# Fixing the place of four small operations on GpSimd and ScalarE from the tenth chunk on

## The chip, the cores and the metric

The kernel runs on one core of a Trainium2 chip. Its five engines (TensorE for matrix products, VectorE, ScalarE, GpSimd, and SyncE, which issues transfers) each work through a list of instructions in a fixed order; they meet only where one waits for another's result. The metric is the device time of one execution in microseconds (us). Before the change it is 552.18 us, the median of three runs (550.71 to 553.72).

## The reference, cut to what matters

Two parts follow each other. The first is a gated linear attention (an mLSTM) over 4 batches, 8 heads and 768 steps with head dimension 40; for each step t

```python
m_new  = maximum(f[t] + m, i[t])
f_stab = exp(f[t] + m - m_new);  i_stab = exp(i[t] - m_new)
C = f_stab * C + i_stab * outer(v[t], k[t])
n = f_stab * n + i_stab * k[t]
y[t] = sigmoid(o_gate[t]) * (C @ q[t]) / maximum(abs(n @ q[t]), 1.0)
```

The second is a dense block over the 3072 rows of y, 320 wide, with 1536 inner columns:

```python
out = ((x @ w_a) * (x @ w_b)) @ w_out
```

## The kernel before, in words

**Chunks.** The 768 steps are cut into six stretches of 128; a stretch of one batch with its eight heads is a chunk, so there are 24 chunks, numbered 0 to 23 in the order stretch by stretch. Batch and stretch of chunk n are `n % 4` and `n // 4`. Inside a chunk the recurrence is written as masked matrix products: scores of queries against keys (`pS`), times a matrix E of decays (one 128 x 128 block for each head), times the values (`pV`), plus a part from the state carried over (`pI`). Products that need full precision are made of several bf16 parts ("high", "middle", "low").

**Steps of one chunk.** The function `attention` goes through the chunks and in each through the letters B, D, E, A, C, U, F:

- B (`stage_b`, twice, for four heads each, then `stage_i`): scores on TensorE (L544), E times the scores on VectorE (L549), its high part cast to bf16 on ScalarE (L551, "the P cast"), the middle and low parts on VectorE (L553, L555); the state's part (L570, L574).
- D (`stage_d`) of the chunk before: the gated result y is transposed on TensorE (L709) and split into two parts (L713, L714), the dense block's input. In every fourth chunk the output gates of the next stretch are loaded here (L208, 4 transfers) and put through a sigmoid on ScalarE (L218).
- E (`stage_e`) of the next chunk: its E begins as a copy of gate sums spread over all partitions (`gbc`, a transfer of 512 KB, issued at L225); GpSimd masks it (L485, one instruction for all heads), ScalarE takes eight exponentials, one for each head (L492).
- A (`stage_a`, then `stage_v`) of the next chunk: queries and keys are split in three parts (L510, L515, L520, L521 on ScalarE, L514, L517 on VectorE), and transposed by transfers that SyncE issues (L524, four for each chunk). Values are split in three parts by two subtractions on GpSimd (L531, then L533).
- C (`stage_c`): values weighted for the state on GpSimd (L584), E times values on TensorE (L603), sums on VectorE and GpSimd (L610, L614).
- U (`stage_u`): the state's update (L630, L637, L641), its parts (L648, L649, L654, L655) and their way through device memory (L658 to L661); it also issues the load of the gate sums two chunks ahead.
- F (`stage_f`): the denominator on VectorE (L671 to L673), the gate times its reciprocal on GpSimd (L686, "the gate's product"), times the numerator on VectorE (L687), and a copy of the last columns on ScalarE (L688).

**The dense block.** Chunks are gathered into nine blocks of two or three (`sizes`); `moe_block` runs twelve inner slices for each: 16 products "up" (L812), then on VectorE and ScalarE a copy, a product and two parts (L818, L819, L821, L823), and, two slices later, the products "down" (L783). While block kb runs through the dense part, the attention of block kb + 2 is traced between its pieces.

**Order.** The start of the kernel is written out in a fixed order. All that follows is put in order on each engine by the compiler's planner, which runs the traced program through a model of the machine and issues what becomes ready there first. The order found there is what the chip then follows, whatever comes late on the chip. `tc.issue_after(x)` adds one constraint: what is traced in the block, on the engine of x, comes behind x in that engine's list. It is an order alone, not a wait.

**Names for the step that is moved.** `after["p"]` is set at L686 and holds the gate's product of the chunk whose F was traced last; before the change it is set and never read. When `stage_e` and `stage_v` of chunk n are traced, in the middle of chunk n - 1, the last F traced is that of chunk n - 2. `stage_b` of chunk n - 1 has already been traced then, with both its P casts.

Of the kernel before, what the change touches and what calls it, by code (L numbers as in the profile page):

```python
# [14 lines left out]
AF = mybir.ActivationFunctionType  # L15
ALU = mybir.AluOpType
# [4 lines left out]
def kernel(  # L21
# [13 lines left out]
    nc = tc.nc  # L35
    B, H, S, D = q.shape
    DM, DFF = w_a.shape
    P = 128
# [54 lines left out]
    for j in range(3):  # L93
# [4 lines left out]
        mask, mask, pattern=[[1, P]], compare_op=ALU.is_ge, fill=-1e30, base=0, channel_multiplier=-1  # L98
# [6 lines left out]
    x = ident[0:BH, 0:BH].rearrange("k (x j) -> k x j", j=2)  # L105
# [20 lines left out]
    after = {}  # L126
# [101 lines left out]
    def top(x):  # L228

        return x.bitcast(BF16).rearrange("p h (d w) -> p h d w", w=2)[:, :, :, 1]  # L230
# [98 lines left out]
    def beta_col(c, b):  # L329
        return g_col(c, b, 0)  # L330
# [149 lines left out]
    def stage_e(n):  # L480

        c, b = chunks[n]
        E = gbc.pop(n)
        st.setdefault(n, {})["E"] = E
        nc.gpsimd.affine_select(  # L485
            E, E, pattern=[[0, H], [1, P]], compare_op=ALU.is_ge, fill=-1e30, base=0,
            channel_multiplier=-1,
        )
        yield
        beta = beta_col(c, b)  # L490
        for h in range(H):
            nc.scalar.activation(E[:, h], E[:, h], AF.Exp, bias=beta[:, h:h + 1])  # L492
            if h % 2 == 1:
                yield

# [32 lines left out]
    def stage_v(n):  # L528
        s = st[n]
        x, vr, vl = (v3[n % NQ][:, i] for i in range(3))  # L530
        nc.gpsimd.tensor_tensor(vr, x, top(x), op=ALU.subtract)  # L531
        yield
        nc.gpsimd.tensor_tensor(vl, vr, top(vr), op=ALU.subtract)  # L533
        yield

    def stage_b(n, hf):
        s = st[n]
        qT, kT = s["T"]
        pS = ps_at.tile([P, HH, P], F32, tag="pat", name=f"pS{n}_{hf}")
        K3 = 3 * D  # L540
        for x in range(HH):
            h = hf * HH + x
            for w in range(2):
                nc.tensor.matmul(  # L544
                    pS[:, x, :], kT[0:K3, w, h, :], qT[0:K3, w, h, :], start=(w == 0), stop=(w == 1)
                )
        yield
        E = s["E"][:, hf * HH:(hf + 1) * HH]
        nc.vector.tensor_tensor(E, pS, E, op=ALU.mult)  # L549
        pb = apool.tile([P, 2, HH, P], BF16, tag="pb", name=f"pb{n}_{hf}")  # L550
        nc.scalar.copy(pb[:, 0], E)  # L551
        yield
        nc.vector.tensor_tensor(E, E, pb[:, 0], op=ALU.subtract)  # L553
        mid = E.bitcast(BF16).rearrange("s h (t w) -> s h t w", w=2)[:, :, :, 1]
        nc.vector.tensor_tensor(pb[:, 1], E, mid, op=ALU.subtract)  # L555
        s[f"pb{hf}"] = (pb[:, 0], mid, pb[:, 1])
        yield
# [108 lines left out]
    def stage_f(n):  # L666
        s = st[n]
        num = s["num"]
        nq = num[:, :, D]
        den = apool.tile([P, H], F32, tag="den", name=f"den{n}")  # L670
        nc.vector.tensor_scalar(den, nq, -1.0, 1.0, op0=ALU.mult, op1=ALU.max)  # L671
        nc.vector.tensor_tensor(den, nq, den, op=ALU.max)
        nc.vector.reciprocal(den, den)  # L673
        yield
        c, b = chunks[n]
        y = osig[c][:, b]
        yv = y[:, 0:DM].rearrange("p (h d) -> p h d", h=H)
        if n < NS:
            t = apool.tile([P, H * DV], F32, tag="tmp", name=f"y{n}")[:, 0:DM]
            t = t.rearrange("p (h d) -> p h d", h=H)  # L680
            nc.vector.tensor_tensor(t, num[:, :, 0:D], den.unsqueeze(2).broadcast_to([P, H, D]), op=ALU.mult)
            nc.vector.tensor_tensor(yv, t, yv, op=ALU.mult)
            nc.scalar.copy(y[:, DM:], y[:, 2 * P:DM])
            s["y"] = y
            return
        after["p"] = [nc.gpsimd.tensor_tensor(yv, yv, den.unsqueeze(2).broadcast_to([P, H, D]), op=ALU.mult).ins]  # L686
        nc.vector.tensor_tensor(yv, num[:, :, 0:D], yv, op=ALU.mult)  # L687
        nc.scalar.copy(y[:, DM:], y[:, 2 * P:DM])  # L688
        s["y"] = y
        yield  # L690
# [31 lines left out]
    def attention():  # L722
        for n in range(NS, NCH):
# [4 lines left out]
            for o in "BDEACUF":  # L728
# [8 lines left out]
                elif o == "B":  # L737
                    yield from stage_b(n, 0)
                    yield from stage_b(n, 1)
                    yield from stage_i(n)  # L740
                elif o == "D":
                    if n > NS:
                        yield from stage_d(n - 1)
                    if n % B == 0 and n > 0:
                        load_o(n // B)
                elif o == "E":
                    if n + 1 < NE:
                        yield from begin_e(n + 1)
                    elif n + 1 < NCH:
                        yield from stage_e(n + 1)  # L750
                elif o == "A":
                    if n + 1 < NCH:
                        yield from stage_a(n + 1)
                        yield from stage_v(n + 1)
                elif o == "U":
                    if NE <= n + 2 < NCH:
                        load_g(n + 2)
                    u = stage_u(n)
                    yield next(u, None)
                    late.append(u)  # L760
                    if len(late) > 2:
                        yield from late.pop(0)
                else:
                    yield from {"C": stage_c, "F": stage_f}[o](n)
# [186 lines left out]
    with tc.tile_pool(name="spool", bufs=3) as spool:  # L951
# [4 lines left out]
        def start():  # L956
# [57 lines left out]
            signs(2)  # L1014
            run(begin_c(1))
            run(stage_f(0))
            words(2)
            run(stage_u(0))
            load(NS + 2)
            weigh(1)  # L1020
            leading(2)
            signs(3)
            run(stage_f(1))
            d0, d1 = stage_d(0), stage_d(1)
            warm = ps_dn.tile([P, 512], F32, tag="pd2", name="warm2")
# [34 lines left out]
    def rest():  # L1060
        if NS < NE:
            yield from begin_e(NS)
        if NS < NF32:
            yield from begin_a(NS)
        else:
            yield from stage_a(NS)
            yield from stage_v(NS)
        if NS >= NE:
            yield from stage_e(NS)
        yield from attention()  # L1070
# [49 lines left out]
```

## Time and profile before

| | |
|---|---|
| median of three runs | 552.18 us (550.71 to 553.72) |
| profiled execution: its own time / span | 551.88 us / 550.1 us |
| granted TensorE clock, mean | 0.994 |
| busy: TensorE, VectorE, ScalarE, GpSimd | 537.8, 411.6, 269.2, 149.5 us |
| masks L485 | 20, 23.4 us busy |
| exponentials L492 | 160 and 5 table loads, 49.4 us busy |
| first subtraction on values L531 | 18, 15.2 us busy |
| gate's product L686 | 22, 18.2 us busy |

The span is the time from the first to the last record of the profile. A row of the timeline gives the start, the duration, the engine, the line of the kernel, the operation and, in square brackets, how long the engine had been idle before it and what ended that. "PE" is TensorE, "PEld" its loading of weights, "DVE" VectorE, "ACT" ScalarE, "POOL" GpSimd, "SPq" SyncE's queue.

### The profile page before, as it was taken

Reading aid. Unit: us, or ns where it says so; the run is one execution under the profiler, and the core shown is the slowest. Engines: PE = TensorE matmul, PEld = TensorE weight load, DVE = VectorE, ACT = ScalarE, POOL = GpSimd, SP = SyncE. Lnnn points to the kernel's source line nnn. Section 1 sums busy time; section 2 is a strip of 40 time slices with the busy share of each in tenths; the row PEclk is TensorE's granted clock in tenths of the full one; section 3 lists DMA queues with packets and bytes.
Section 4 is the critical chain, followed back from the end, with each engine's and each line's share of the span. In section 5 each row is a group of like instructions: output and inputs, shape, how many; then the busy total and the mean of one; then the engine's idle time right before and its main releaser. Section 6 shows DMA issues by size and latency. Waiting matters only on the chain.

```text
span 550.1 us, 11947 instructions
## 1 busy us (share of the span) xinstructions
PE 537.8 (98%) x4493; PEld 511.4 (93%) x4493; DVE 411.6 (75%) x906; ACT 269.2 (49%) x645; POOL 149.5 (27%) x224
## 2 busy tenths in 40 slices
PE   8999999899999999999999999999999899999997
PEld 5888888799999999999999999999999899999996
DVE  6889999977768785988868974988677846964332
ACT  5574488664425853645625664655354813321111
POOL 3102324545032340442233340444041203210000
PEclk9799999999999999999999999999999999999999
DMA  9999943284537665668646885758459403300001
GB/s 190 217 220 284 323 88 71 64 179 113 89 100 142 139 128 113 133 131 179 121 119 115 127 161 116 140 123 170 91 130 183 102 1 104 78 1 24 1 1 36
DMA packets 198549, 66.71 MB, mean 121 GB/s; under 512 B 184220, under 2 KB 191772, under 8 KB 198492
## 3 DMA queue, kind: packets, MB, share of 16 engines
q1 hardware_dynamic: 198444, 65.86, 56.6%
q8 instruction: 35, 0.57, 0.5%
q14 instruction: 22, 0.18, 0.1%
q10 hardware_dynamic: 48, 0.10, 0.0%
HBM read 41.11 MB, written 5.95 MB: 86 GB/s over the span
## 4 chain that ended last, share of the span: by engine, by line
PE 80%; DVE 6%; DMA 4%; ACT 4%; issue 2%; SPq 2%; POOL 0%; ACTq 0%; DVEq 0%; POOLq 0%
PE pu L812 42%; PE pd L783 20%; PE pU L630 3%; PE pV L603 3%; PE pS L544 3%; DMA T<-qks 2%; DMA osig<-in_o_gate_dram 1%; PE pX L709 1%; PE pV L929 1%; ACT gbc L492 1%; PE pI L570 1%; PE pS L886 1%; PE warm L961 1%; SPq L524 1%; PE pc L451 1%
## 5 line engine op out<-in xcount | busy, mean ns | idle before, releaser
L812 PE MATMUL pu<-xh,w 128*128 128x384 f32 (+1 forms) x1080 | 273.2, 322 | 1.5 <-DVE w L459 0.7
L812 PE MATMUL pu<-xl,w 128*128 128x384 f32 (+1 forms) x648 | 206.1, 320 | 0.0
L812 PEld LDWEIGHTS pu<-xh,w 128*128 128x128 f32 x1080 | 188.3, 188 | 4.0 <-DVE w L459 1.3
L783 PE MATMUL pd<-w,gh 128*128 128x320 f32 x576 | 127.2, 311 | 0.2 <-DVE gh L821 0.2
L812 PEld LDWEIGHTS pu<-xl,w 128*128 128x128 f32 x648 | 121.8, 188 | 0.0
L819 DVE TENSOR_TENSOR g<-pu,g 128x384 f32<-128x384 f32 (+1 forms) x108 | 54.4, 504 | 82.8 <-PE pu L812 47.6
L783 PEld LDWEIGHTS pd<-w,gh 128*128 128x128 f32 x576 | 96.3, 188 | 0.6 <-DVE gh L821 0.4
L818 ACT COPY g<-pu 128x384 f32<-128x384 f32 (+1 forms) x90 | 39.6, 440 | 103.3 <-PE pu L812 96.0
L783 PE MATMUL pd<-w,gl 128*128 128x320 f32 x288 | 84.7, 311 | 0.0
L614 POOL TENSOR_TENSOR num<-v,num 128x168 f32<-128x168 f32 x36 | 21.3, 593 | 210.3 <-DVE v L610 209.7
L823 DVE TENSOR_TENSOR gl<-g,gh 128x384 fp32r<-128x384 f32 (+1 forms) x92 | 57.3, 622 | 2.0
L492 ACT ACTIVATE gbc<-gbc,gtab 128x128 f32<-128x128 f32 x160 | 49.4, 390 | 12.3 <-POOL gbc L485 12.2
L783 PEld LDWEIGHTS pd<-w,gl 128*128 128x128 f32 x288 | 52.7, 188 | 0.2
L821 DVE CAST gh<-g 128x384 fp32r<-128x384 f32 (+1 forms) x108 | 42.2, 390 | 1.7
L515 ACT CAST qks<-r 128x320 bf16<-128x320 f32 x36 | 16.4, 458 | 30.1 <-DVE r L514 30.0
L610 DVE TENSOR_REDUCE v<-pV 128x168 f32<-128x504 f32 x36 | 24.1, 675 | 9.2 <-PE pV L603 9.1
L485 POOL TENSOR_SCALAR_AFFINE_SELECT gbc<-gbc 128x1024 f32<-128x1024 f32 x20 | 23.4, 1171 | 24.7 <-DMA gbc<-g_dram 23.3
L584 POOL TENSOR_TENSOR vw<-va,gtab 128x336 f32<-128x336 f32 x20 | 17.0, 852 | 47.5 <-PE pU L630 22.2
L553 DVE TENSOR_TENSOR gbc<-gbc,pb 128x512 f32<-128x512 f32 x36 | 25.4, 707 | 4.5 <-ACT pb L551 4.5
L520 ACT COPY qks<-qks 128x640 bf16<-128x640 bf16 x36 | 26.1, 725 | 0.7
L549 DVE TENSOR_TENSOR gbc<-pS,gbc 128x512 f32<-128x512 f32 x36 | 24.3, 679 | 1.7 <-PE pS L544 1.7
L551 ACT CAST pb<-gbc 128x512 bf16<-128x512 f32 x36 | 22.2, 617 | 5.7 <-DVE gbc L549 5.6
(152 smaller groups left out, 810.1 us busy)
## 6 DMA issues: line engine op xcount, KB each, us to landing
gbc<-g_dram SPq DMA_DIRECT2D x20, 512.0 KB
q<-in_q_dram SPq DMA_DIRECT2D x24, 160.0 KB
k<-in_k_dram SPq DMA_DIRECT2D x24, 160.0 KB
va<-in_v_dram SPq DMA_DIRECT2D x24, 160.0 KB
osig<-in_o_gate_dram SPq DMA_DIRECT2D x24, 160.0 KB
raw<-in_moe_w_out_dram SPq DMA_DIRECT2D x12, 320.0 KB
out_dram<-o SPq DMA_DIRECT2D x24, 160.0 KB
raw<-in_moe_w_a_dram SPq DMA_DIRECT2D x8, 384.0 KB
```

Source lines behind the costliest of these rows:

```text
L485: nc.gpsimd.affine_select(E, E, pattern=[[0, H], [1, P]], compare_op=ALU.is_ge, fill=-1e30, base=0, channel_multiplier=-1,)
L492: nc.scalar.activation(E[:, h], E[:, h], AF.Exp, bias=beta[:, h:h + 1])
L520: nc.scalar.copy(qks[:, 0, :, lo:lo + 2 * D], qks[:, 1, :, D - lo:3 * D - lo])
L549: nc.vector.tensor_tensor(E, pS, E, op=ALU.mult)
L553: nc.vector.tensor_tensor(E, E, pb[:, 0], op=ALU.subtract)
L610: nc.vector.tensor_reduce(t, pv.rearrange("p h i d -> p h d i"), axis=mybir.AxisListType.X, op=ALU.add)
L783: nc.tensor.matmul(pd[t][:, 0:DM], a[:, cols], w, start=(ff == 0 and first), stop=(ff == NF - 1 and last),)
L812: nc.tensor.matmul(acc[j], a, r, start=(x == 0), stop=(x == len(terms) - 1),)
L818: (nc.vector.tensor_copy if ff in [1, 2] else nc.scalar.copy)(g, acc[0])
L819: nc.vector.tensor_tensor(g, acc[1], g, op=ALU.mult)
L821: nc.vector.tensor_copy(gh, g)
L823: (nc.gpsimd if kb * 12 + ff < 16 else nc.vector).tensor_tensor(gl, g, gh.bitcast(F32), op=ALU.subtract)
```

## The change

From chunk 9 on (`n > 2 * B`, B = 4, so for the fifteen chunks 9 to 23) three things are put in a fixed place in their engine's list. The mask of chunk n (L485) and the first subtraction on its values (L531) are issued on GpSimd behind the gate's product of chunk n - 2. The eight exponentials of chunk n (L492) are issued on ScalarE behind the P cast of the second four heads of chunk n - 1 (L551). No instruction is added or taken away, and all data, waits and buffers are as before.

```diff
@@ stage_e(n)
-        nc.gpsimd.affine_select(
-            E, E, pattern=[[0, H], [1, P]], compare_op=ALU.is_ge, fill=-1e30, base=0,
-            channel_multiplier=-1,
-        )
+
+        fixed = n > 2 * B
+        with tc.issue_after(after["p"]) if fixed else nullcontext():
+            nc.gpsimd.affine_select(
+                E, E, pattern=[[0, H], [1, P]], compare_op=ALU.is_ge, fill=-1e30, base=0,
+                channel_multiplier=-1,
+            )
         yield
         beta = beta_col(c, b)
         for h in range(H):
-            nc.scalar.activation(E[:, h], E[:, h], AF.Exp, bias=beta[:, h:h + 1])
+            with tc.issue_after(after["pb"]) if fixed else nullcontext():
+                nc.scalar.activation(E[:, h], E[:, h], AF.Exp, bias=beta[:, h:h + 1])
@@ stage_v(n)
-        nc.gpsimd.tensor_tensor(vr, x, top(x), op=ALU.subtract)
+        with tc.issue_after(after["p"]) if n > 2 * B else nullcontext():
+            nc.gpsimd.tensor_tensor(vr, x, top(x), op=ALU.subtract)
@@ stage_b(n, hf)
-        nc.scalar.copy(pb[:, 0], E)
+        after["pb"] = nc.scalar.copy(pb[:, 0], E).ins
@@ stage_f(n)
-        after["p"] = [nc.gpsimd.tensor_tensor(yv, yv, den.unsqueeze(2).broadcast_to([P, H, D]), op=ALU.mult).ins]
+        after["p"] = nc.gpsimd.tensor_tensor(yv, yv, den.unsqueeze(2).broadcast_to([P, H, D]), op=ALU.mult).ins
```

## The prediction

> **What bounds the kernel now.** I read the page's busy shares first.
>
> ```profile
> PE 537.8 (98%) x4493; PEld 511.4 (93%) x4493; DVE 411.6 (75%) x906; ACT 269.2 (49%) x645; POOL 149.5 (27%) x224
> ```
>
> TensorE (PE) is busy for 98% of the span. The change touches GpSimd (27%) and ScalarE (49%) alone, and only from chunk 9, whose mask is the sixth on GpSimd's timeline:
>
> ```profile
> 162.78 1.36 POOL L485 TENSOR_SCALAR_AFFINE_SELECT gbc<-gbc 128x1024 f32<-128x1024 f32 x1 [1.22 <-DMA gbc<-g_dram]
> ```
>
> So the question is how much PE is idle behind that point. The table of busy time by stretch answers it; the first column is PE, and the other engines follow.
>
> ```profile
> core 0: us, PE busy (x) PEld busy (x) DVE busy (x) ACT busy (x) POOL busy (x), PEclk, DMA share, GB/s
> 160.00:240.00 80.00, 80.00 (x703) 76.78 (x702) 65.68 (x136) 43.69 (x105) 27.09 (x38) 1.00 0.64 134
> 240.00:260.00 20.00, 19.41 (x175) 18.52 (x175) 16.23 (x34) 12.75 (x29) 8.64 (x13) 1.00 0.80 165
> 260.00:420.00 160.00, 160.00 (x1366) 154.99 (x1363) 123.22 (x260) 83.53 (x206) 48.91 (x65) 1.00 0.68 131
> 420.00:440.00 20.00, 18.55 (x146) 17.95 (x145) 16.64 (x33) 14.87 (x32) 6.17 (x8) 1.00 0.63 138
> 460.00:480.00 20.00, 19.81 (x212) 19.04 (x211) 19.48 (x48) 8.24 (x22) 7.66 (x10) 1.00 0.42 101
> 480.00:500.00 20.00, 20.00 (x168) 19.94 (x168) 11.82 (x29) 5.12 (x13) 1.82 (x3) 1.00 0.05 18
> ```
>
> PE is idle for 20 - 19.41 = 0.59 us, then 20 - 18.55 = 1.45 us, then 20 - 19.81 = 0.19 us: together 2.23 us, 0.4% of the time, in all the stretch where attention work is left for the change to move. The clock is at 1.00 in each. Everything else that PE lost lies ahead of chunk 9. The view of who waited for whom, for PE, names the three places:
>
> ```profile
> PE pX L709 <- DVE gbc L549: 1.4, 1, 1.4
> PE pS L544 <- DMA T<-qks: 1.1, 2, 0.6
> PE pd L783 <- DVE gh L821: 0.2, 1, 0.2
> ```
>
> **The change part by part.** It adds no instruction, no transfer and no wait; fifteen masks, fifteen subtractions and 120 exponentials get a later place. A typical chunk from the timelines of GpSimd, VectorE and ScalarE, at chunk 13's E (the product belongs to chunk 11, the casts to chunk 12):
>
> ```profile
> 242.56 1.21 POOL L485 TENSOR_SCALAR_AFFINE_SELECT gbc<-gbc 128x1024 f32<-128x1024 f32 x1 [1.45 <-DMA gbc<-g_dram]
> 243.75 1.02 POOL L686 TENSOR_TENSOR osig<-osig,den 128x320 f32<-128x320 f32 x1
> 242.00 0.18 DVE L673 RECIPROCAL den<-den 128x8 f32<-128x8 f32 x1
> 244.11 0.68 DVE L549 TENSOR_TENSOR gbc<-pS,gbc 128x512 f32<-128x512 f32 x1
> 245.74 0.68 DVE L549 TENSOR_TENSOR gbc<-pS,gbc 128x512 f32<-128x512 f32 x1
> 262.93 0.68 DVE L549 TENSOR_TENSOR gbc<-pS,gbc 128x512 f32<-128x512 f32 x1
> 243.81 2.46 ACT L492 ACTIVATE gbc<-gbc,gtab 128x128 f32<-128x128 f32 x8 [1.02 <-POOL gbc L485]
> 246.75 0.61 ACT L551 CAST pb<-gbc 128x512 bf16<-128x512 f32 x1
> 247.79 0.62 ACT L551 CAST pb<-gbc 128x512 bf16<-128x512 f32 x1
> ```
>
> *The mask and the subtraction.* The denominator is ready at 242.00 + 0.18 = 242.18, but the product runs at 243.75, since the mask stands in front of it and itself waited 1.45 us for its transfer. Behind the change the product can run at 242.2: 1.55 us earlier. The mask then ends near 242.2 + 1.02 + 1.21 = 244.4 instead of 243.77, so 0.7 us later. What waited behind the mask was the product, and behind that VectorE's L687 and ScalarE's copy L688; what is late next is the exponentials. The subtraction L531 stood behind the product here already.
>
> *The exponentials.* They start at 243.81 and hold ScalarE for 2.46 us; behind them queue the next keys' cast (L510), both P casts and L688. VectorE finishes the first product with E at 244.11 + 0.68 = 244.79, so the first cast can come some 2 us earlier, and with it L553 and L555. The exponentials move behind the second cast, to about 245.74 + 0.68 + 0.62 = 247.0, and end at 249.5. Who waits for them is the next chunk's L549, at 262.93: 13 us of cover. Were that gone, the cost would be what the exponentials are late by, 249.5 - 246.27 = 3.2 us, in each chunk, and PE would only pay it where it has no dense products to run.
>
> So in each chunk a chain of small operations gets 1.5 to 2.5 us shorter, and PE, which is full, gains nothing from it. The gain can come at the three idle places only.
>
> *First place, 0.59 us.* PE waits for chunk 13's transposes. From the timelines of SyncE's queue and ScalarE:
>
> ```profile
> 249.02 2.71 SPq L208 DMA_DIRECT2D osig<-in_o_gate_dram  x4
> 251.77 5.54 SPq L524 DMA_TRANSPOSE T<-qks  x3
> 255.47 1.28 ACT L218 ACT_TABLE_LOAD   x1 [4.96 <-DMA osig<-in_o_gate_dram]
> ```
>
> Three transposes stand behind the four gate loads. Both hang on work that the exponentials hold up (the loads on chunk 11's y, transposes on the keys' parts). If both start the 1.5 to 2.5 us earlier that was found above, the 0.59 us go. The exponentials' new time, 247 to 249.5, lies ahead of the 4.96 us in which ScalarE idles for the gates. Bounds: 0 where the queue's order stays and the loads are no earlier, -0.59. I take -0.59, as 1.5 us is well over it.
>
> *Second place, 1.45 us.* PE waits at 431 us for VectorE's L549, which frees the score bank:
>
> ```profile
> 427.12 0.72 POOL L686 TENSOR_TENSOR osig<-osig,den 128x320 f32<-128x320 f32 x1 [2.37 <-ACT osig L218]
> 427.79 1.09 POOL L485 TENSOR_SCALAR_AFFINE_SELECT gbc<-gbc 128x1024 f32<-128x1024 f32 x1
> 431.93 0.68 DVE L549 TENSOR_TENSOR gbc<-pS,gbc 128x512 f32<-128x512 f32 x1
> ```
>
> Here the mask already stands behind the product, which was late because of the sigmoid (2.37 us of waiting), and this L549 waits for no exponential of the next chunk. The change removes nothing in front of it. Bounds 0 and -1.45; I take 0.
>
> *Third place, 0.19 us, and the fifteenth chunk.* In the narrow block near 465 us VectorE is busy for 19.48 of 20 us, and PE waits for its L821:
>
> ```profile
> 463.46 1.35 POOL L485 TENSOR_SCALAR_AFFINE_SELECT gbc<-gbc 128x1024 f32<-128x1024 f32 x1 [1.56 <-DMA gbc<-g_dram]
> 464.79 0.74 POOL L531 TENSOR_TENSOR va<-va 128x336 f32<-128x336 f32 x1
> 465.61 1.08 POOL L533 TENSOR_TENSOR va<-va 128x336 f32<-128x336 f32 x1
> 467.89 1.06 POOL L686 TENSOR_TENSOR osig<-osig,den 128x320 f32<-128x320 f32 x1 [1.21 <-DVE den L673]
> 476.76 0.69 DVE L549 TENSOR_TENSOR gbc<-pS,gbc 128x512 f32<-128x512 f32 x1 [0.28 <-PE pS L544]
> ```
>
> Here the mask and both subtractions ran 3 us ahead of the product and now come behind it, from 468.95 to 468.95 + 1.35 + 0.74 + 1.08 = 472.1. Chunk 23's exponentials follow the mask and end near 470.3 + 2.46 = 472.8, still 4 us ahead of the L549 that needs them. While GpSimd works, VectorE is slower (rows at rival A). With GpSimd quiet until 467.9, VectorE reaches L821 earlier and PE's 0.19 us go; the slowness comes again behind 469. Bounds -0.19 and +3.17 (the three operations' whole time laid on PE); I take -0.19, as the table shows no idle PE in the 20 us that follow.
>
> **Sum:** 551.88 - 0.59 - 0 - 0.19 = 551.10 us for the profiled execution. That execution lies 0.30 us under the median of the runs shown (552.18), so the median should be 551.4.
>
> **The rivals.** *A: GpSimd's work lands on a full VectorE.* Two rows show what one mask does to VectorE:
>
> ```profile
> 304.30 1.25 POOL L485 TENSOR_SCALAR_AFFINE_SELECT gbc<-gbc 128x1024 f32<-128x1024 f32 x1 [1.41 <-DMA gbc<-g_dram]
> 304.64 1.32 DVE L823 TENSOR_TENSOR gl<-g,gh 128x384 fp32r<-128x384 f32 x1
> 296.61 0.56 DVE L823 TENSOR_TENSOR gl<-g,gh 128x384 fp32r<-128x384 f32 x1
> ```
>
> L823 begins inside the mask, ends at 305.96, 0.41 us behind the mask's end at 305.55, and takes 1.32 instead of 0.56 us. Where VectorE has no slack, such a delay reaches PE through L821 and L823. It has none near 470 us, where the change puts 3.17 us of GpSimd's work: 551.88 + 3.17 + 0.30 = 555.35 us. It decides where VectorE's lateness passes what PE has in hand, and PE already waits for L821 in this stretch. Against it: the same 3.17 us are taken from 463 to 467, so the load is only moved. The Trainium skill (SBUF — State Buffer, "SBUF: two separate sides") says that the two engines share one pair of ports as an exclusive lock, held for a whole instruction, while the other blocks; by that rule the mask costs VectorE up to its full duration wherever it lands, and the sum would be this rival's. The rows just shown agree with the lock.
>
> *B: PE's pieces come together in other ways.* When both score halves run at once they cost less than apart. From the chain in order of time and PE's timeline:
>
> ```profile
> 242.67 0.91 PE pS L544 x16
> 285.33 0.55 PE pS L544 x8
> 289.51 0.46 PE pS L544 x8
> 305.17 0.42 PE L812 MATMUL pu<-xh,w 128*128 128x384 f32 x1
> 306.64 0.34 PE L812 MATMUL pu<-xh,w 128*128 128x384 f32 x1
> ```
>
> Apart: 0.55 + 0.46 = 1.01 against 0.91, and one more first "up" product behind a switch, 0.42 against 0.34: 0.18 us a chunk, at most 2.7 us for fifteen. With an earlier cast and E used sooner, the planner may draw the halves together. With half of that and all three idle places gone: 551.88 - 2.23 - 1.35 + 0.30 = 548.6 us. Against it: PE's order depends on much that the change does not touch, and it may as well part halves that are together now.
>
> *C: the shift is swallowed.* The chains get shorter, the queue's order in front of PE does not change, all three waits stay: 552.2 us. For it: the two waits that matter end on transposes and on VectorE, neither of which the change moves itself.
>
> **How the numbers follow.** About 0.5% (2.8 us) is what a measurement of this kernel can tell from no change, its three runs being 3 us apart. The forecast has 0.42, C 0.15: both within 0.5%. B has 0.18 and is faster, since the three idle places alone (0.4%) do not get there. A, and any order of the planner that leaves PE waiting as long, has 0.25 and is slower. The range goes from a little under B (548.3) to a little over A (555.6); the likeliest case's own is 549.9 (all 2.23 us) to 552.8.
>
> **What would show it.** Product L686 ahead of mask L485 on GpSimd in all fifteen chunks, and no longer held by the mask's transfer; eight exponentials behind two P casts, and the casts right behind L549; no PE wait on transposes near 258 us; the 1.4 us wait of L709 still there; PE busy near 538 us. The forecast is wrong if PE's idle time behind 160 us grows past 4 us (then A, with waits on L821 or L819, or a new one), or if PE's busy time itself falls by over 1 us (B).

## The result, and the profile after

The changed kernel is slower: a median of 555.09 us (553.25 to 558.74) against 551.94 us (549.95 to 554.93) for the kernel before, fourteen runs of each. The ratio is 1.006, with a 95% interval of 1.0036 to 1.0085. Executions that took far longer than the rest are left out of every ratio, and f1 below has no idle time because its profile is of such an execution. The profiled execution took 555.12 us, its span 553.3 us.

In the rows from here on the lines of the kernel stand three to five higher than before: mask L488, exponentials L496, subtractions L536 and L538, scores L549, E times scores L554, P cast L556, middle and low parts L558 and L560, product of the gate L691, numerator L692, casts of the transposed y L718 and L719, transposes of y L714, "down" L788, "up" L817, the dense block's copy L823, and its two parts L826 (gh) and L828 (gl).

The page of the changed kernel, busy time by engine:

```profile
PE 536.6 (97%) x4493; PEld 509.1 (92%) x4493; DVE 417.2 (75%) x906; ACT 270.6 (49%) x645; POOL 152.0 (27%) x224
```

No engine has more instructions, yet VectorE is busy for 5.6 us more. TensorE (PE) is what sets the time, so the table of busy time by stretch comes next, with the columns shown before (behind the length of the stretch, the first is PE and the sixth the granted clock):

```profile
160.00:240.00 80.00, 78.45 (x673) 75.22 (x672) 63.99 (x130) 44.07 (x105) 27.09 (x35) 1.00 0.60 132
240.00:260.00 20.00, 20.00 (x193) 18.83 (x192) 18.58 (x40) 9.79 (x25) 9.18 (x14) 1.00 0.64 133
260.00:420.00 160.00, 159.34 (x1352) 153.40 (x1352) 125.14 (x260) 84.93 (x202) 51.08 (x67) 1.00 0.64 133
420.00:440.00 20.00, 19.52 (x161) 18.54 (x159) 15.44 (x30) 14.63 (x32) 6.31 (x8) 1.00 0.80 159
440.00:460.00 20.00, 19.40 (x125) 19.40 (x126) 7.76 (x16) 4.84 (x13) 0.00 (x0) 1.00 0.00 1
460.00:480.00 20.00, 19.27 (x197) 18.52 (x196) 17.88 (x40) 8.22 (x22) 7.00 (x9) 1.00 0.49 125
```

PE's idle time from 160 to 480 us is 1.55 + 0 + 0.66 + 0.48 + 0.60 + 0.73 = 4.02 us, where it was 2.23 us. Place by place, in PE's timeline: the 0.59 us near 258 are gone and the 1.45 near 431 are down to 0.22; 1.52 near 203, 0.66 near 273 and 0.86 near 440 (it begins before 440 and so falls into two stretches) are new, and the 0.19 near 469 have become 0.73 near 472. The view of who waited for whom names what PE waits for there:

```profile
PE pX L714 <- DVE gbc L554: 1.7, 2, 1.5
PE pu L817 <- ACT g L823: 1.5, 2, 0.9
PE pd L788 <- DVE gh L826: 0.7, 1, 0.7
```

The second row is a wait that the kernel before did not have in this part: PE waits for ScalarE's copy of an "up" product. The timelines of ScalarE, TensorE and VectorE show why, first near 273 us (exponentials of chunk 14), then near 440 (chunk 22):

```profile
269.05 1.28 ACT L496 ACT_TABLE_LOAD   x1
270.34 2.47 ACT L496 ACTIVATE gbc<-gbc,gtab 128x128 f32<-128x128 f32 x8
272.72 0.45 ACT L519 CAST qks<-r 128x320 bf16<-128x320 f32 x1
273.06 0.47 ACT L823 COPY g<-pu 128x384 f32<-128x384 f32 x1
...
273.59 0.45 PE L817 MATMUL pu<-xh,w 128*128 128x384 f32 x1 [0.66 <-ACT g L823]
...
289.35 0.68 DVE L554 TENSOR_TENSOR gbc<-pS,gbc 128x512 f32<-128x512 f32 x1
...
436.06 1.28 ACT L496 ACT_TABLE_LOAD   x1
437.36 2.47 ACT L496 ACTIVATE gbc<-gbc,gtab 128x128 f32<-128x128 f32 x8
439.73 0.44 ACT L514 CAST qks<-q 128x320 bf16<-128x320 f32 x1
440.08 0.47 ACT L823 COPY g<-pu 128x384 f32<-128x384 f32 x1
...
440.60 0.44 PE L817 MATMUL pu<-xh,w 128*128 128x384 f32 x1 [0.86 <-ACT g L823]
```

The eight exponentials stand as one block behind the second P cast. For a chunk that follows a sigmoid, a load of ScalarE's function table (ACT_TABLE_LOAD) stands in front of them: together 3.8 us. Behind the block stands the copy that empties a bank (a buffer that PE's products land in) of "up" products, and PE wants that bank. The row of VectorE shows the first product that needs chunk 14's exponentials, 16 us behind their end.

The wait near 203 us is on VectorE (timelines of VectorE and TensorE, the changed kernel, then the same two before):

```profile
199.65 0.62 PE L549 MATMUL pS<-T,T 120*128 120x128 bf16 x8
...
200.07 0.68 DVE L554 TENSOR_TENSOR gbc<-pS,gbc 128x512 f32<-128x512 f32 x1
...
201.43 1.03 DVE L692 TENSOR_TENSOR osig<-num,osig 128x320 f32<-128x320 f32 x1
202.38 1.23 DVE L558 TENSOR_TENSOR gbc<-gbc,pb 128x512 f32<-128x512 f32 x1
203.54 0.68 DVE L554 TENSOR_TENSOR gbc<-pS,gbc 128x512 f32<-128x512 f32 x1
...
204.27 0.55 PE L714 MATMUL pX<-ident,osig 128*128 128x128 f32 x3 [1.52 <-DVE gbc L554]
```

```profile
200.87 1.07 PE L544 MATMUL pS<-T,T 120*128 120x128 bf16 x16
...
203.87 1.27 DVE L549 TENSOR_TENSOR gbc<-pS,gbc 128x512 f32<-128x512 f32 x2
...
206.20 0.53 PE L709 MATMUL pX<-ident,osig 128*128 128x128 f32 x3
```

Before, the planner had put both halves of E times the scores together, and both halves of the scores on PE. Now two slow operations stand between the halves on VectorE. The second half, which frees the score bank, ends no later than before (204.22 against 205.14 us), but PE, whose list is redrawn too, has issued its scores earlier and comes for the bank earlier: at 206.20 us before, from 202.75 on after. So it is the two lists together that make this wait. Near 472 us it is the late product of the gate and GpSimd's work behind it (timelines of GpSimd, VectorE, TensorE, changed kernel):

```profile
469.39 0.86 POOL L691 TENSOR_TENSOR osig<-osig,den 128x320 f32<-128x320 f32 x1 [4.83 <-DVE den L678]
470.21 1.54 POOL L488 TENSOR_SCALAR_AFFINE_SELECT gbc<-gbc 128x1024 f32<-128x1024 f32 x1
...
470.72 1.57 DVE L558 TENSOR_TENSOR gbc<-gbc,pb 128x512 f32<-128x512 f32 x1
472.21 0.83 DVE L826 CAST gh<-g 128x256 fp32r<-128x256 f32 x1
...
473.10 0.70 PE L788 MATMUL pd<-w,gh 128*128 128x320 f32 x3 [0.73 <-DVE gh L826]
```

The mask lies on VectorE's L558, which takes 1.57 us there against 0.68 in most chunks, and gh comes late behind it. That the mask is what makes gh late is read from these rows and was not tried alone: e2 below, where the mask is free, waits 1.20 us for the same cast.

### The profile page after: what moved, and what is told of

Same layout as the page of the kernel before. It is cut to its first block, busy times and chain, and to the rows that moved or that the text cites. A ratio compares the mean times of both kernels' runs of the same rounds, so it can differ in the third digit from the quotient of the medians.

```text
span 553.3 us, 11941 instructions
## 1 busy us (share of the span) xinstructions
PE 536.6 (97%) x4493; PEld 509.1 (92%) x4493; DVE 417.2 (75%) x906; ACT 270.6 (49%) x645; POOL 152.0 (27%) x224
## 4 chain that ended last, share of the span: by engine, by line
PE 71%; DVE 11%; ACT 5%; issue 5%; DMA 4%; SPq 2%; POOL 1%; ACTq 0%; DVEq 0%; POOLq 0%
PE pu L817 40%; PE pd L788 19%; PE pV L608 3%; PE pS L549 2%; PE pU L635 2%; ACT gbc L496 1%; DVE cw L425 1%; PE pX L714 1%; DMA osig<-in_o_gate_dram 1%; DVE cr L428 1%; DMA T<-qks 1%; DMA c_dram<-cb 1%; DVE w L459 1%; PE pI L575 1%; DVE gh L826 1%
## 5 line engine op out<-in xcount | busy, mean ns | idle before, releaser
L817 PE MATMUL pu<-xh,w 128*128 128x384 f32 (+1 forms) x1080 | 273.8, 323 | 3.2 <-ACT g L823 1.5
L817 PE MATMUL pu<-xl,w 128*128 128x384 f32 (+1 forms) x648 | 206.4, 321 | 0.0
L817 PEld LDWEIGHTS pu<-xh,w 128*128 128x128 f32 x1080 | 188.0, 188 | 6.0 <-ACT g L823 2.1
L788 PE MATMUL pd<-w,gh 128*128 128x320 f32 x576 | 126.5, 310 | 0.7 <-DVE gh L826 0.7
L817 PEld LDWEIGHTS pu<-xl,w 128*128 128x128 f32 x648 | 121.8, 188 | 0.1
L788 PEld LDWEIGHTS pd<-w,gh 128*128 128x128 f32 x576 | 96.3, 188 | 1.1 <-DVE gh L826 0.9
L788 PE MATMUL pd<-w,gl 128*128 128x320 f32 x288 | 84.5, 311 | 0.0
L823 ACT COPY g<-pu 128x384 f32<-128x384 f32 (+1 forms) x90 | 39.7, 441 | 86.0 <-PE pu L817 78.6
L828 DVE TENSOR_TENSOR gl<-g,gh 128x384 fp32r<-128x384 f32 (+1 forms) x92 | 52.3, 568 | 1.5
L788 PEld LDWEIGHTS pd<-w,gl 128*128 128x128 f32 x288 | 52.6, 188 | 0.4 <-DVE gl L828 0.2
L496 ACT ACTIVATE gbc<-gbc,gtab 128x128 f32<-128x128 f32 x160 | 49.6, 393 | 3.9 <-POOL gbc L488 3.9
L826 DVE CAST gh<-g 128x384 fp32r<-128x384 f32 (+1 forms) x108 | 45.4, 420 | 1.6
L558 DVE TENSOR_TENSOR gbc<-gbc,pb 128x512 f32<-128x512 f32 x36 | 28.8, 801 | 4.4 <-ACT pb L556 4.4
L556 ACT CAST pb<-gbc 128x512 bf16<-128x512 f32 x36 | 22.2, 619 | 15.5 <-DVE gbc L554 15.5
L488 POOL TENSOR_SCALAR_AFFINE_SELECT gbc<-gbc 128x1024 f32<-128x1024 f32 x20 | 24.6, 1228 | 11.6 <-DMA gbc<-g_dram 10.3
L691 POOL TENSOR_TENSOR osig<-osig,den 128x320 f32<-128x320 f32 x22 | 17.7, 805 | 29.2 <-DVE den L678 18.8
```

The lines of the kernel that those rows point to most:

```text
L488: nc.gpsimd.affine_select(E, E, pattern=[[0, H], [1, P]], compare_op=ALU.is_ge, fill=-1e30, base=0, channel_multiplier=-1,)
L556: after["pb"] = nc.scalar.copy(pb[:, 0], E).ins
L788: nc.tensor.matmul(pd[t][:, 0:DM], a[:, cols], w, start=(ff == 0 and first), stop=(ff == NF - 1 and last),)
L817: nc.tensor.matmul(acc[j], a, r, start=(x == 0), stop=(x == len(terms) - 1),)
L823: (nc.vector.tensor_copy if ff in [1, 2] else nc.scalar.copy)(g, acc[0])
L826: nc.vector.tensor_copy(gh, g)
```

## The experiments

The first four kernels leave the order to the compiler's planner. The others have the list of every engine written out, taken from the kernel before or from the changed one, so that nothing moves but what the experiment moves. "Idle" in the table is PE's idle time from 160 to 480 us, 320 us less PE's busy time in that stretch of each profile. Each ratio is to runs of the kernel before on the same chip.

| kernel | median us | ratio (95%) | idle us |
|---|---|---|---|
| before | | 1 | 2.23 |
| the change | 555.09 | 1.0060 (1.0036 to 1.0085) | 4.02 |
| e1: masks and subtractions | 556.62 | 1.0075 (1.0039 to 1.0112) | 4.31 |
| e2: exponentials | 555.18 | 1.0058 (1.0037 to 1.0078) | 4.21 |
| e3: masks | 556.33 | 1.0082 (1.0061 to 1.0103) | 3.55 |
| e5: the change, exponentials of 10, 14, 18, 22 free | 558.26 | 1.0121 (1.0101 to 1.0140) | 4.88 |
| r1: lists of before, all moves | 559.48 | 1.0136 (1.0113 to 1.0160) | 7.77 |
| r1a: lists of before, GpSimd's moves | 564.23 | 1.0225 (1.0191 to 1.0259) | 9.85 |
| r1b: lists of before, exponentials | 555.31 | 1.0063 (1.0041 to 1.0086) | 4.35 |
| r2: lists after, moves put back | 577.75 | 1.0463 (1.0432 to 1.0494) | 16.23 |
| f1: r1b without chunks 14, 18, 22 | 551.38 | 0.9979 (0.9953 to 1.0006) | – |
| f2: r1b, chunks 14, 18, 22 alone | 556.21 | 1.0079 (1.0052 to 1.0107) | 4.11 |
| f3: r1 without four places | 553.42 | 1.0018 (0.9992 to 1.0045) | 2.98 |
| f4: the change, copy ahead at two places | 552.95 | 1.0014 (0.9991 to 1.0036) | 2.27 |
| f5: f4 and two repairs on VectorE | 553.90 | 1.0019 (0.9990 to 1.0049) | 2.59 |
| f6: f1 and one repair on VectorE | 552.96 | 0.9999 (0.9972 to 1.0026) | 2.05 |

### Parts of the change, as the planner draws them

e1 frees the exponentials, e2 frees mask and subtraction, e3 keeps the mask's constraint alone, and e5 takes the constraint from the exponentials that follow a sigmoid:

```diff
 e1, e3
-            with tc.issue_after(after["pb"]) if fixed else nullcontext():
+            with tc.issue_after(after["pb"]) if False else nullcontext():
 e2 (both), e3 (the subtraction's)
-        with tc.issue_after(after["p"]) ...
+        with tc.issue_after(after["p"]) if False else nullcontext():
 e5
-            with tc.issue_after(after["pb"]) if fixed else nullcontext():
+            with tc.issue_after(after["pb"]) if fixed and n % B != 2 else nullcontext():
```

> Masks and values' first subtractions of chunks 9 to 23 behind the gate's product as in the change; the exponentials free, as before. Theory G (GpSimd's mask and subtractions now run while VectorE is full, and slow it until TensorE waits): 2 to 3.5 us slower than before, with a wait of TensorE on VectorE near 470 us, and VectorE's busy time up by 3 us or more. Theory S (the exponentials, with the table load ahead of them, stand as one block of 2.5 to 3.75 us behind the second P cast and in front of the dense block's copies on ScalarE): no more than 1 us from before, and no wait of TensorE on ScalarE's copy.

> Exponentials of chunks 9 to 23 behind the second P cast as in the change; masks and subtractions free, as before. Theory S: 2 to 3.5 us slower than before, with TensorE waiting on ScalarE's copy g twice, about 0.8 and 1.0 us. Theory G: within 1 us of before, VectorE's busy time as before to 1 us.

> The masks alone behind the gate's product; subtractions and exponentials free. Theory G: slower by 1 us or more, since the mask is the longest of the three operations that move; Theory S: within 1 us of before. If the slowness comes from any new order the planner draws rather than from one part, this run has waits of TensorE at places that none of the others has.

> The whole change, but the exponentials of chunks 10, 14, 18 and 22, those that follow a sigmoid and need a table load of 1.28 us first, stay free. Theory S: the two waits of TensorE on ScalarE's copy (0.82 and 1.03 us) are gone, and the time is 1.5 to 2 us under that of the change. Theory G: as slow as the change to 0.7 us.

Each part alone costs about what the whole costs, so the parts don't add up, and e5, meant to take a cost away, is the slowest of the four. The waits lie at other places in each kernel: a constraint makes the planner draw all five lists anew. e1 came out as theory G had it (0.73 us of waiting near 472, VectorE busy for 4.0 us more). e2 has the time that theory S gave but not its waits: none is on the dense block's copy; one of 1.17 us near 437 is on ScalarE's copy L693 (L688 before), which stands behind chunk 22's block there. With the planner in between, these runs can't tell a part from its redrawing.

### The moves without the new order, and the new order without the moves

r1 keeps the lists of before and moves 25 instructions of GpSimd (13 masks, and the subtractions that stood ahead of the product; two masks stood behind it already) and 120 exponentials of ScalarE to where the change puts them. r1a and r1b each do one engine. r2 takes the lists of the changed kernel, with every mask back ahead of the product and the exponentials ahead of the first P cast. The edits for one chunk, as line numbers in an engine's list:

```diff
 r1, r1b: ScalarE, chunk 14
-L525 L519 L524 L693 exp*2 L556 exp*4 L823 exp*2 L653 L514 L556 L525 L519
+L525 L519 L524 L693 L556 L823 L653 L514 L556 exp*8 L525 L519
 r1, r1a: GpSimd, chunk 23
-L488 L536 L538 L691
+L691 L488 L536 L538
```

> Every engine's list is written out by hand as it is in the kernel before, on TensorE, VectorE and SyncE without any change; on GpSimd alone the masks (and the subtractions, where they stood ahead) are put behind the gate's product, on ScalarE alone the exponentials behind the second P cast, for chunks 9 to 23. So these are the change's moves without the order that the planner drew around them. Theory M (the moves themselves cost: GpSimd on a full VectorE, exponentials in front of copies): 2 to 3.5 us slower than before. Theory P (the cost is the order that the planner draws anew for TensorE, VectorE and SyncE): within 1 us of before, with TensorE's waits behind 160 us 3 us or less in sum.

> Every engine's list is written out by hand as it is in the changed kernel, but with each mask of chunks 9 to 23 put back in front of the gate's product on GpSimd, and each chunk's exponentials in front of the first P cast on ScalarE. So this is the new order of TensorE, VectorE and SyncE without the moves. Theory P: 2 to 4 us slower than before, like the change; some more is possible, since the lists were drawn for the other places. Theory M: within 1 us of before.

> As the lists of before with the moves alone, but only GpSimd's (25 instructions change their place), ScalarE as before. Theory M with GpSimd as the cause: 1.5 us or more slower than before, and a wait on VectorE near 470 us of 0.8 us or more. Theory P: within 1 us, VectorE's busy time within 2 us of before.

> As the lists of before with the moves alone, but only ScalarE's (120 exponentials), GpSimd as before. Theory M with ScalarE as the cause: 1.5 us or more slower than before, with waits on ScalarE's copy near 270 and 440 us. Theory P: within 1 us of before; the wait on transposes near 258 us may shrink.

The moves by themselves cost 7.6 us (559.48 against 551.92), more than the change. So the theory that only the redrawn order costs has fallen: the new order takes back more than half of what the moves cost. It does not fit the old placement, as r2 shows (25.8 us slower; why so much was not followed up). Neither theory had these sizes: r1 lies above the 2 to 3.5 us of theory M, r2 far above the 2 to 4 of theory P. In r1 PE's longest waits are on ScalarE's copy. The view of waits, then the timelines of ScalarE and GpSimd near chunk 23:

```profile
PE pu L817 <- ACT g L823: 3.7, 3, 2.3
```

```profile
469.30 0.62 ACT L556 CAST pb<-gbc 128x512 bf16<-128x512 f32 x1
473.31 2.45 ACT L496 ACTIVATE gbc<-gbc,gtab 128x128 f32<-128x128 f32 x8 [3.40 <-POOL gbc L488]
475.66 0.35 ACT L823 COPY g<-pu 128x256 f32<-128x256 f32 x1
...
471.12 1.06 POOL L691 TENSOR_TENSOR osig<-osig,den 128x320 f32<-128x320 f32 x1 [4.83 <-DVE den L678]
472.14 1.14 POOL L488 TENSOR_SCALAR_AFFINE_SELECT gbc<-gbc 128x1024 f32<-128x1024 f32 x1
```

GpSimd stands idle for 4.83 us until the denominator is there, because the mask, which could run, is now behind the product. ScalarE stands idle for 3.40 us, because the exponentials wait for the mask. The copy behind them starts as they end. PE pays for both.

### Where the exponentials' cost sits

f1 and f2 divide r1b: f1 leaves the exponentials of chunks 14, 18 and 22 where they were and moves the other twelve; f2 moves those three alone.

```diff
-for n in range(9, 24): move the exponentials of n behind the second P cast
+f1: for n in range(9, 24) if n not in (14, 18, 22)
+f2: for n in (14, 18, 22)
```

> Every engine keeps the list of the kernel before; only the exponentials of twelve chunks move behind the second P cast (not those of 14, 18 and 22, behind which the dense block's copy or the cast of x stood when all fifteen moved). Theory Q (an instruction that frees a bank of TensorE stands behind the moved block): the waits near 269 (1.5 us), 360 (1.2) and 439 us (0.6) are gone, and the 0.9 us wait on transposes near 258 stays gone, so the time is that of before within 1.5 us, 550.5 to 552.5. Rival S (the later exponentials slow VectorE and the chain everywhere, the three waits are only where it shows): 12 of 15 parts of the 3.4 us loss stay, 554 to 555.

> The complement: lists of before, and only the exponentials of chunks 14, 18 and 22 move. Theory Q: the three waits come back (about 1.5 + 1.2 + 0.6 = 3.3 us) and the wait of 0.9 us near 258 stays as before, so about 555 us. Rival S: a fifth of the loss, 552 to 553.

Twelve blocks cost nothing that can be measured (0.9979), three cost 0.8%. f6 below moves the same twelve blocks, and its profile shows none of the three waits. The wait on transposes near 258, which f2 was expected to keep, is gone there. The view of waits of f2 shows the copy of g, and xl (L719), which follows the cast of x (L718); that cast stands behind chunk 18's block:

```profile
PE pu L817 <- ACT g L823: 1.3, 2, 0.9
PE pV L608 <- DVE xl L719: 1.0, 1, 1.0
```

These three chunks follow a sigmoid (chunk 10 does too, but has no such wait), so their block is 3.8 instead of 2.5 us long. Whether the shorter block would do no harm at the same three places was not tried.

### The changed kernel with the copy ahead

f4 has the lists of the changed kernel, and f5 adds two edits on VectorE:

```diff
 f4, f5: ScalarE, chunk 14
-L556 exp*8 L519 L823
+L556 L823 exp*8 L519
 f4, f5: ScalarE, chunk 22
-L556 exp*8 L514 L823
+L556 L823 exp*8 L514
 f5: VectorE, chunk 10
-L554 L828 L692 L558 L554
+L554 L828 L554 L692 L558
 f5: VectorE, near 470 us
-L521 L560 L558 L826
+L521 L826 L560 L558
```

> Every engine keeps the list of the changed kernel; on ScalarE alone the next copy of an up product goes ahead of the exponentials of chunks 14 and 22. Theory Q: TensorE's waits on that copy (0.8 us near 273 and 1.0 near 439) go and nothing comes in their place, as the exponentials have 10 us in hand: 1.9 us less than the changed kernel, about 553.2. Rival S: the waits move to the next copy or to VectorE and the time stays at 555.

> As the kernel with the copy ahead, and on VectorE, in chunk 10, the second product of E with the scores (which frees the score bank that TensorE waits for, 1.8 us near 202) goes ahead of the numerator's product and one subtraction, and near 470 us the cast of gh (0.9 us of TensorE's waiting) ahead of two instructions of the P parts. Theory Q: 0.8 + 1.0 + 1.5 + 0.9 = 4.2 us less than the changed kernel, about 551, that is the time of before: the whole loss sits at four places. Rival S: VectorE is busy for 5.6 us more than before and hands the lateness on to whatever comes next, so under 2 us come back, 553 or more.

Two instructions moved past sixteen exponentials bring the changed kernel back to the time of before. f4's timeline of ScalarE at chunk 14, and its row for 160 to 480 us:

```profile
267.41 0.61 ACT L556 CAST pb<-gbc 128x512 bf16<-128x512 f32 x1
267.93 0.47 ACT L823 COPY g<-pu 128x384 f32<-128x384 f32 x1
268.42 1.28 ACT L496 ACT_TABLE_LOAD   x1
269.71 2.46 ACT L496 ACTIVATE gbc<-gbc,gtab 128x128 f32<-128x128 f32 x8
```

```profile
160.00:480.00 320.00, 317.73 (x2719) 306.21 (x2719) 251.48 (x518) 166.14 (x397) 100.76 (x133) 1.00 0.60 126
```

The copy could run at 267.93 and had stood at 273.06, and PE's idle time is 2.27 us against 2.23 us before. f5's edits did take the wait near 203 away, but others of 0.8 and 1.1 us in sum came near 354 and 434 us, and the 0.73 us near 472 became two waits of 0.47 and 0.12: the lateness is handed on, as the rival had it, and no gain over f4 can be measured.

### GpSimd's share, and a try at a faster kernel

f3 is r1 without the blocks of chunks 14, 18 and 22 and without any move of chunk 23. f6 is f1 with one edit against the 1.4 us wait near 431 us.

```diff
 f3: not moved
+exponentials of 14, 18, 22; mask, subtractions and exponentials of 23
 f6: VectorE, near 431 us
-L826 L521 L521 L554
+L826 L554 L521 L521
```

> Lists of the kernel before on all engines; mask, subtractions and exponentials move as in the change, but for the exponentials of chunks 14, 18 and 22 and all of chunk 23. Theory Q (GpSimd's share of the loss is the copy held up near 473 us): of the 7.6 us that all the moves cost, the waits near 269, 360, 441 and 473 (1.0 + 2.0 + 0.6 + 2.5 us, and about 1.5 us of slower matmuls behind the last) are gone, and the time is 551 to 553. Rival S (GpSimd's later work slows VectorE in every chunk): the 4.2 us between the moves on both engines and the exponentials alone stay for the most part, 555 or more.

> Lists of before, exponentials moved in twelve chunks as above, and on VectorE, near 431 us, the product of E with the scores that frees the score bank goes ahead of two subtractions of the keys' parts (0.88 us). Theory Q: of the 1.4 us for which TensorE waits there, 0.9 go, and nothing else changes: about 0.9 us under the kernel without the three blocks, 550.5, and under before. Rival S: the wait passes to the transposes of the keys behind those subtractions or to the next cast, and the time stays at 551.4.

In f3 the masks and subtractions of fourteen chunks stand behind the product (twelve of the masks were moved there), and eleven blocks of exponentials behind the casts, and that costs nothing that can be measured. So of r1's 7.6 us nearly all sat at four places. GpSimd's part of it is chunk 23, where the product is late by itself. This holds with the exponentials moved as well. In r1a they keep their old place, ahead of the P casts and the copy, and wait there for the later mask (5.13 us near 474); PE's waits on the copy are 4.9 us, and the loss is 12.3 us, which was not taken apart further. f6 did not come under the kernel before: the wait at 431 shrank, and one for gl of the same size came 2.3 us later. The view of waits of f6:

```profile
PE pX L714 <- DVE gbc L554: 0.6, 1, 0.6
PE pd L788 <- DVE gl L828: 0.6, 1, 0.6
```

No kernel here is measurably faster than before.

## Why the prediction was wrong, step by step

*What bounds the kernel* was right: PE sets the time, and PE's idle time behind 160 us goes broadly with the ratio in the table. From it the prediction drew that only the three idle places could change. That holds for a gain. A loss needs no idle place: it makes one, wherever an instruction that frees a bank for PE comes late.

*The exponentials* are the step that failed. The prediction asked who waits for the exponentials, found "13 us of cover", and named what was queued behind them at their old place (L510, the P casts, L688); the P casts now stand ahead of the block in every chunk. It did not ask what would be queued behind them at the new place. That was the dense block's copy at chunks 14 and 22, for which PE had no cover. f4 prices this step: with the lists of all other engines left alone, the two waits of 0.66 and 0.86 us go, PE's idle time falls by 1.75 us (4.02 to 2.27), and no loss is left that can be measured (1.0014, 0.9991 to 1.0036). The price that the prediction set for lost cover, "3.2 us in each chunk", hung on the next L549, which never waited for them (they end 5.1 us or more ahead of it in every chunk), and the table load of 1.28 us was in no term.

*The mask and the subtraction.* The product comes ahead of the mask in all fifteen chunks, as forecast, but not all of them are moved: 13 of the 15 masks and 7 of the 15 first subtractions stood ahead of it before. Twelve of the fifteen blocks are free in f1, and fourteen of the fifteen masks in f3. "What is late next is the exponentials" was right, and at chunk 23 in r1 that was one link of the wait of 2.3 us; the other, the copy behind the exponentials, is the same failed step.

*First place* (-0.59): the number came right, PE is busy for 20.00 of 20 us, but the reason is not shown. In f2 the exponentials of chunks 11 to 13 keep their place, the gate loads and the three transposes start as before (249.07 and 251.90 us, against 249.02 and 251.77), and the wait is gone all the same. In r1b the loads start 1.24 us earlier, but PE comes to the scores 1.25 us earlier too. So this is luck. *Second place* (0): 1.23 of its 1.45 us went, by the lists that the planner drew anew; with the lists of before, in r1b, 1.19 us stay. The prediction had no step for that. *Third place* (-0.19): wrong, it grew by 0.54 us, at rival A's place, with a sixth of its price and, as far as the rows show, by its mechanism. Rival A's 555.35 us is near the measured 555.09 by accident, since f4 still has its wait near 470 and the time of before. The prediction gave 0.25 to a slower kernel, for A or for any order of the planner that leaves PE waiting as long; that chance covers what came out, not the step that made it so.

The prediction's rule of the Trainium skill (SBUF — State Buffer, "SBUF: two separate sides") made rival A the sum: by the lock, as the prediction read it, the mask costs VectorE up to its duration wherever it lands. (The Trainium skill has the lock only for VectorE's operations in a 2-port mode or, against an operation of GpSimd that reads SBUF, with two inputs from SBUF.) The rows agree with the lock (L558 at 1.57 us beside the mask) and the page's busy time of VectorE rose by 5.6 us, but the time did not follow: f4's VectorE is busy 416.0 us, 4.4 us over before, and f4 is within 0.4% of before. So nearly all of that longer work costs PE nothing; near 472 us it may.

*Near 203 us* the planner parted two halves that stood together, on PE and on VectorE. Rival B had the planner regroup PE's pieces, for a gain, and named the parting as what speaks against it; what counted was a wait of 1.52 us. In sum the changed lists lose 1.52 + 0.66 + 0.86 + 0.54 and gain 0.59 + 1.23, 1.76 of the 1.79 us of PE's idle time. So the failed step is 1.52 us of it; the wait near 203 is as large, and the gain near 431 nearly makes up for that one. From PE's 420th "up" product, near 160 us, to the 1500th, near 490, the profiled executions differ by 2.7 us; 1.79 of them are idle time, and for 0.9 us PE is busy longer over the same number of products, which was not taken apart. 0.5 us of the span's 3.2 us lies ahead of that, where both run the same order.

*The sign of B* (PE's busy time down by over 1 us) is there on the page, 537.8 to 536.6 us, and does not mean B: all of the fall lies ahead of the 420th "up" product, where the change does nothing, and behind it PE's busy time rises by 0.9 us. In the first 40 us the granted clock was 0.91 before and 1.00 after, and PE was busy for 37.73 and 36.79 us.

## What to carry to other kernels

To cost an instruction that moves later, list what stands behind it in its engine's queue at the new place, and who waits for those, with the same care as who waits for the instruction itself; a block of eight counts with its table load as one. An instruction that can run, put behind one that waits for another engine, costs where that wait is long: the mask behind the product was free in fourteen chunks and not in the one whose product was late. And where a planner draws the order, part-by-part trials move everything at once: write the lists out, move only what is in question, and compare idle time of the engine that sets the time.

## What the runs showed of the hardware

A wait of PE can cost more than its own length. In r1 PE waits 1.87 us near 362 us and over 2 us near 475, and the granted clock falls afterwards. r1's timeline of PE, then its busy time in stretches of 2 us (behind the length, the first number is PE, the sixth the clock):

```profile
362.31 0.22 PE L608 MATMUL pV<-va,pb 128*128 128x126 bf16 x1 [1.87 <-DVE xl L719]
```

```profile
362.00:364.00 2.00, 1.68 (x28) 1.58 (x27) 1.93 (x5) 0.04 (x1) 1.00 (x2) 0.86 0.97 218
364.00:366.00 2.00, 2.00 (x8) 1.92 (x7) 1.80 (x6) 0.48 (x1) 1.76 (x4) 0.50 0.77 226
366.00:368.00 2.00, 2.00 (x12) 2.00 (x11) 1.22 (x4) 1.18 (x2) 0.33 (x1) 0.79 1.22 218
...
474.00:476.00 2.00, 0.00 (x0) 0.00 (x0) 2.00 (x3) 2.00 (x9) 1.10 (x2) 1.00 0.27 59
476.00:478.00 2.00, 1.93 (x9) 1.94 (x10) 1.68 (x5) 1.05 (x4) 0.00 (x0) 0.52 0.06 14
478.00:480.00 2.00, 2.00 (x13) 1.96 (x11) 1.09 (x4) 0.48 (x1) 0.00 (x0) 0.63 0.99 223
480.00:482.00 2.00, 2.00 (x26) 1.96 (x25) 0.99 (x3) 0.37 (x1) 0.00 (x0) 1.00 0.12 25
```

If the clock is either full or half, PE spends (0.14 + 0.50 + 0.21) x 2 / 0.5 = 3.4 us after the first wait and (0.48 + 0.37) x 2 / 0.5 = 3.4 us after the second at half clock, and loses half of each, 1.7 us. Together that is an estimated 3.4 us of this one execution; the clocks of r1's five executions differ (0.988 to 0.994) and their times do not follow, so it is no share of the median. A wait of 1.72 us in f3 left the clock at 1.00 (timeline of PE and stretch, f3):

```profile
437.77 0.55 PE L714 MATMUL pX<-ident,osig 128*128 128x128 f32 x3 [1.72 <-DVE gbc L554]
```

```profile
438.00:440.00 2.00, 2.00 (x15) 1.96 (x14) 1.56 (x4) 2.00 (x7) 0.00 (x0) 1.00 0.97 220
```

The Trainium skill (TensorE: Matmul & The Clock Gate, "HAM oscillation — how this bites in real kernels") tells to avoid idle gaps of PE over about 3.4 us. The slow stretch here is as long as that figure, which the Trainium skill gives for the gap; the slow stretches here follow gaps of 1.87 us and 2.33 us. The length of the gap alone does not decide: in r2 the clock stays at 1.00 after a gap of 1.79 us near 320 us, and after one of 1.78 us near 455 us it is 0.59 and 0.56 in two stretches of 2 us. What does decide stays open.
